# Attention and two mixing FFN layers on one core: token blocks taken layer by layer, weight conversion moved into PSUM and through HBM

## The chip, the cores and the metric

The kernel runs on one core of a Trainium2 chip. The metric is the device time of one execution in microseconds (us), median of the runs; the profile is one execution with the hardware profiler on.

## The reference, cut to what matters

Inputs are float32 for q, k, v, s and the norm's gain, and float64 for the weights (w_ch1, w_ch2 of both layers, U and V). Everything is computed to about float32 precision.

```python
def reference(...):                       # B, H, S, D = 4, 8, 576, 64; d_model 512, FFN 2048
    # causal attention with a bias from a cumulative sum of max(s, 0)
    scores = q @ k.T / 8 + minimum(-(cum_i - cum_j), 0);  attn = softmax(causal(scores)) @ v
    x = concat of the heads               # (4, 576, 512)
    # layer 0
    xn = layer_norm(x) * g_ln
    x = x + maximum(xn @ w_ch1, 0) @ w_ch2
    # layer 1: tokens are mixed with rank 32 first
    u = x + (x.T @ U @ V).T
    return u + maximum(u @ w_ch1b, 0) @ w_ch2b
```

## The kernel before

**Blocks, tiles, steps.** Each of the 4 batches has two token blocks: A (256 tokens) and B (320). A layer's FFN of one block is 16 steps, one for each tile m of 128 hidden units; 2 layers x 8 blocks x 16 = 256 steps. A step is `mlp1` (w1 tile by the normalised tokens, PSUM tile ps) and, LAG = 2 steps later, `mlp2` (w2 tile by the hidden tokens, summed in PSUM over the 16 tiles). To keep float32 precision at the fast matmul format, each operand is split in a high and a low part and three products are made (lines 1026 to 1028 and 1060 to 1062); a step has 24 matmuls of 256 or 320 columns. Between the two, ACT makes hh (L1032) and DVE hl (L1033). The first two steps (FULL_STEPS) run in full precision instead.

**Order of the blocks.** `GROUPS` lists them: A0, A1, A2, B0, A3 in layer 0, then A0 with B0 in layer 1, B1, B2 in layer 0, A1 with B1 in layer 1, and so on. A group takes its first eight tiles for all its blocks, then the other eight; the next group of the layer starts with the eight tiles that are still in SBUF (WSLOTS = 8).

**Attention** of a block (`attn_items`) is spread over the steps given in `AT`, its layer norm (`layer_norm`) comes at the step in `LN`. A0 comes before everything. After layer 0 a block's tokens are mixed with U (`t_items`) and go to HBM (x_dr, t_dr); before its layer 1 they come back (`u_load`, `u_items`). Attention inputs of all blocks but A0 and A1 are first copied within HBM (`bounce`).

**Weights.** A tile has two halves (w1, w2), each 128 x 512 float64 values: 512 KB raw, and 512 KB as high and low part. `w_raw` loads a half into one of three buffers wr. `f64_to_f32` (L460) turns it into float32 in a buffer wt: ACT scales the high word (L466), DVE shifts it left (L469), ACT scales the low word (L471), DVE puts the sign in (L473), POOL adds the low word (L476). `split` then makes the high part w (L352 on ACT or L353 on DVE) and the difference (L357 on DVE or L359 on POOL). `w_split` does this for each half when its turn comes, straight into the w slot that the step uses; a half that is needed again is stored to HBM (w_dr, L519), and later uses load it back from there (L507). 72 halves are converted, 216 loaded back.

**What sets the order.** All work is recorded as operations with an engine (or several to choose from), a priority (the step) and buffers. `Plan.issue` plans them once with prices for each operation, and writes out a fixed order for each engine; every DMA is issued from SP's queue, in that order. Each engine runs its list in order and waits where an operand or a buffer is not ready. PSUM has eight banks: two acc, six ps.

Of the kernel before, what the change touches and what calls it, by code (L numbers as in the profile page):

```python
# [1203 lines left out]
```

## Time and profile before

| | |
|---|---|
| median of 3 runs | 1158.63 us (1158.39 to 1163.0) |
| profiled execution | 1164.62 us, its span 1162.8 us |
| mean granted TensorE clock | 0.973 |
| busy: PE, DVE, ACT, POOL | 1096.6, 618.9, 518.1, 251.3 us |
| matmuls | 7817 |
| DMA | 264.86 MB, 68.8% of 16 engines' span |

Rows of matmuls are longer than the distance between their starts, since they run pipelined; the distance is what a matmul costs. A stretch view gives, for each engine, the time in which it was busy and in brackets how many instructions; "PEclk" is the granted clock as a share of full speed, "DMA" the mean busy share of the 16 DMA engines. Waits are put down to who came last.

### The profile page before, as it was taken

The page shows a single profiled execution, that of the slowest core. Times are in us where ns is not written, and L with a number is a line of the kernel's source. Part 1 is how long each engine was busy: PE and PEld are TensorE (multiplying, and loading weights), DVE is VectorE, ACT ScalarE, POOL GpSimd, SP SyncE. Part 2 cuts the span into 40 slices and gives each one's busy share as a digit, 9 for nine tenths or more (in the row PEclk, how much of TensorE's full clock was granted, in tenths as well). Part 3 has the DMA queues.
Part 4 walks back from the last instruction along what each step waited for, and adds up shares of the span by engine and source line. Part 5 has one row for each costly group of instructions (what it writes and reads, how often), then busy time and mean ns, then how long its engine had stood idle before and what let it go on. Part 6 is the DMA issues. An engine that isn't in the chain of part 4 may idle for free.

```text
span 1162.8 us, 21147 instructions
## 1 busy us (share of the span) xinstructions
PE 1096.6 (94%) x7817; PEld 1035.6 (89%) x7817; DVE 618.9 (53%) x1463; ACT 518.1 (45%) x1212; POOL 251.3 (22%) x391
## 2 busy tenths in 40 slices
PE   8897888999999988798999999999999999999998
PEld 5685788989899987797899989989899999999998
DVE  6877878755554568767845463463441133223122
ACT  7677676645543467556644353342331121112111
POOL 4444344302201144433511030110010000000000
PEclk9998798999999999799899999999999999999999
DMA  7799889596485898869879928955617983611621
GB/s 215 240 358 318 260 271 321 176 274 234 158 302 162 238 336 283 294 221 337 277 245 311 314 63 252 378 188 140 229 47 276 371 284 109 205 46 46 212 79 41
DMA packets 122535, 264.86 MB, mean 228 GB/s; under 512 B 42592, under 2 KB 60544, under 8 KB 122304
## 3 DMA queue, kind: packets, MB, share of 16 engines
q1 hardware_dynamic: 122432, 263.50, 68.8%
q8 instruction: 62, 1.02, 0.3%
q14 instruction: 41, 0.34, 0.1%
HBM read 218.13 MB, written 61.05 MB: 240 GB/s over the span
## 4 chain that ended last, share of the span: by engine, by line
PE 66%; DMA 16%; ACT 5%; DVE 5%; issue 5%; SPq 2%; POOL 2%; POOLq 0%; DVEq 0%; ACTq 0%
PE ps L1026 9%; PE ps L1028 9%; PE ps L1027 9%; PE acc L1060 6%; PE acc L1062 6%; PE acc L1061 6%; DMA t<-cum_dr 4%; PE ps L761 3%; DMA wr<-w1b 3%; PE ps L1062 3%; PE ps L1060 3%; PE ps L1061 3%; PE ps L714 3%; PE ps L665 2%; DMA w<-w_dr 2%
## 5 line engine op out<-in xcount | busy, mean ns | idle before, releaser
L1026 PE MATMUL ps<-xh,w 128*128 128x256 f32 (+1 forms) x1016 | 315.6, 311 | 15.2 <-ACT w L352 5.5
L1027 PE MATMUL ps<-xh,w 128*128 128x256 f32 (+1 forms) x1016 | 306.3, 301 | 7.1 <-DVE w L357 6.9
L1028 PE MATMUL ps<-xl,w 128*128 128x256 f32 (+1 forms) x1016 | 305.4, 301 | 3.4 <-POOL xl L359 3.1
L1033 DVE SCALAR_TENSOR_TENSOR hl<-ps,hh 128x256 fp32r<-128x256 f32 (+1 forms) x254 | 115.6, 455 | 309.9 <-ACT hh L1032 308.7
L1032 ACT ACTIVATE hh<-ps 128x256 fp32r<-128x256 f32 (+1 forms) x254 | 103.3, 407 | 375.2 <-PE ps L1028 373.1
L1060 PE MATMUL acc<-hh,w 128*128 128x256 f32 (+1 forms) x760 | 233.0, 307 | 3.8 <-ACT hh L1032 3.5
L1061 PE MATMUL acc<-hh,w 128*128 128x256 f32 (+1 forms) x760 | 225.7, 297 | 5.1 <-DVE w L357 4.7
L1062 PE MATMUL acc<-hl,w 128*128 128x256 f32 (+1 forms) x760 | 225.9, 297 | 1.1 <-DVE hl L1033 1.1
L1026 PEld LDWEIGHTS ps<-xh,w 128*128 128x128 f32 x1016 | 197.1, 194 | 23.0 <-issue 6.9
L1027 PEld LDWEIGHTS ps<-xh,w 128*128 128x128 f32 x1016 | 197.2, 194 | 9.4 <-DVE w L357 8.8
L1028 PEld LDWEIGHTS ps<-xl,w 128*128 128x128 f32 x1016 | 197.3, 194 | 4.1 <-POOL xl L359 3.5
L1060 PEld LDWEIGHTS acc<-hh,w 128*128 128x128 f32 x760 | 147.8, 195 | 9.5 <-ACT hh L1032 5.0
L1061 PEld LDWEIGHTS acc<-hh,w 128*128 128x128 f32 x760 | 148.2, 195 | 6.8 <-DVE w L357 5.6
L1062 PEld LDWEIGHTS acc<-hl,w 128*128 128x128 f32 x760 | 148.1, 195 | 2.3 <-DVE hl L1033 2.0
L476 POOL TENSOR_TENSOR wt<-wt,wr 128x512 int32<-128x512 int32 (+2 forms) x71 | 98.9, 1393 | 138.1 <-DVE wt L473 78.0
L675 ACT ACTIVATE t<-t,mx 128x256 f32<-128x256 f32 (+4 forms) x144 | 83.2, 579 | 46.1 <-DVE mx L669 28.7
L615 POOL TENSOR_SCALAR_AFFINE_SELECT t<-t 128x128 f32<-128x128 f32 (+2 forms) x128 | 47.7, 378 | 168.6 <-DMA t<-cum_dr 148.3
L1062 PE MATMUL ps<-hl,w 128*128 128x320 f32 x256 | 79.1, 309 | 0.0
L1061 PE MATMUL ps<-hh,w 128*128 128x320 f32 x256 | 79.1, 309 | 0.0
L1060 PE MATMUL ps<-hh,w 128*128 128x320 f32 x256 | 79.1, 309 | 0.0
L714 PE MATMUL ps<-ident,t 128*128 128x128 f32 x400 | 65.4, 280 | 10.3 <-ACT t L688 5.4
L357 DVE TENSOR_TENSOR pB<-ps,pB 128x512 fp32r<-128x512 f32 (+1 forms) x96 | 53.9, 575 | 30.5 <-ACT pB L352 29.6
(137 smaller groups left out, 1585.0 us busy)
## 6 DMA issues: line engine op xcount, KB each, us to landing
w<-w_dr SPq DMA_DIRECT2D x216, 512.0 KB, 6.8
w_dr<-w SPq DMA_DIRECT2D x64, 512.0 KB, 6.1
t<-cum_dr SPq DMA_DIRECT2D x60, 192.0 KB, 6.1
wr<-w1a SPq DMA_DIRECT2D x20, 512.0 KB, 5.6
wr<-w2a SPq DMA_DIRECT2D x20, 512.0 KB, 5.7
t<-cum_dr SPq DMA_DIRECT2D x32, 256.0 KB, 6.2
wr<-w1b SPq DMA_DIRECT2D x16, 512.0 KB, 6.6
wr<-w2b SPq DMA_DIRECT2D x16, 512.0 KB, 5.9
```

The lines of the kernel that those rows point to most:

```text
L357: alts = {"dve": (68 + 1.042 * n, lambda: nc.vector.tensor_tensor(out=out(), in0=a(), in1=b(), op=op))}
L476: P.op(prio, {"pool": (148 + 2.104 * n, lambda: nc.gpsimd.tensor_tensor(out=dst().bitcast(I32), in0=dst().bitcast(I32), in1=pair(0).bitcas ...
L675: act(prio, K, lambda t=t, mx=mx, o=o, K=K, x=x, y=nt * z + x: nc.scalar.activation(t[:, o:o + K], t[:, o:o + K], AF.Exp, bias=mx[:, (1 if ...
L714: nc.tensor.transpose(ps[:, 128 * j:128 * (j + 1)], t[:, c:c + 128], ident.tile)
L1026: nc.tensor.matmul(ps[:, :n], w[:, 0, sl], xh[:, k, :n], start=k == 0, stop=False)
L1027: nc.tensor.matmul(ps[:, :n], w[:, 1, sl], xh[:, k, :n], start=False, stop=False)
L1028: nc.tensor.matmul(ps[:, :n], w[:, 0, sl], xl[:, k, :n], start=False, stop=k == KT - 1)
L1032: act(st - 1000, n, lambda: nc.scalar.activation(hh[:, :n], ps[:, :n], AF.Relu), [ps], [hh], 51)
L1033: dve(st - 1000, n, lambda: nc.vector.scalar_tensor_tensor(out=hl[:, :n], in0=ps[:, :n], scalar=0.0, in1=f(hh[:, :n]), op0=ALU.max, op1=AL ...
L1060: nc.tensor.matmul(a, w[:, 0, sl], hh[:, :n], start=new, stop=False)
L1061: nc.tensor.matmul(a, w[:, 1, sl], hh[:, :n], start=False, stop=False)
L1062: nc.tensor.matmul(a, w[:, 0, sl], hl[:, :n], start=False, stop=last and (z == 1 or blk == "B"))
```

## The change

All blocks go through layer 0 first, A0 and A1 together, then one by one; layer 1 follows in four pairs. Attention of all blocks lies before step 100 now (before: 168), and no step runs in full precision.

The first eight tiles are converted straight into w, as before, and always stored. All other tiles are converted ahead by the new `w_ahead`: raw half into wr (four buffers now), converted, split back into the same wr buffer, stored to HBM; every use in a step is then a load from HBM. The other tiles of layer 0 come at steps 6 to 8, those of layer 1 between steps 37 and 123.

The conversion works in a PSUM bank (one of the six ps) in place of wt: ACT scales the high word into PSUM, ACT scales the low word, one DVE pass shifts and ORs the low word in, one puts the sign in, and the split reads PSUM (so POOL can't take the difference). POOL's add falls away. The v part of the attention inputs is loaded straight into buffers xs and no longer copied in HBM first. The planner's DMA rate is 330 instead of 360 bytes per ns.

```diff
-FULL_STEPS = 2
-
-GROUPS = ((0, "A0"), (0, "A1"), (0, "A2"), (0, "B0"), (0, "A3"), (1, "A0", "B0"), (0, "B1"), (0, "B2"),
-          (1, "A1", "B1"), (0, "B3"), (1, "A2", "B2"), (1, "A3", "B3"))
-
-AT = {"A1": (0, 11), "A2": (11, 24), "B0": (24, 45), "A3": (45, 60), "B1": (64, 100), "B2": (100, 126), "B3": (126, 168)}
-LN = {"A1": 11, "A2": 26, "B0": 45, "A3": 61, "B1": 109, "B2": 127, "B3": 174}
+FULL_STEPS = 0
+
+GROUPS = ((0, "A0", "A1"), (0, "A2"), (0, "A3"), (0, "B0"), (0, "B1"), (0, "B2"), (0, "B3"),
+          (1, "A0", "B0"), (1, "A1", "B1"), (1, "A2", "B2"), (1, "A3", "B3"))
+
+AT = {"A2": (0, 8), "A3": (18, 34), "B0": (26, 48), "B1": (45, 61), "B2": (66, 87), "B3": (76, 100)}
+LN = {"A2": 16, "A3": 36, "B0": 60, "B1": 65, "B2": 90, "B3": 102}
+W0 = (6, 2)
+W1 = (37, 123)
...
-    sb("w", dict(w=2 * WSLOTS, wr=3, wt=2))
+    sb("w", dict(w=2 * WSLOTS, wr=4))
...
-        it["fresh"], it["keep"] = k not in seen, False
-        if k in seen:
-            inst[seen[k]]["keep"] = True
-            if k not in w_dr:
-                w_dr[k] = P.fixed(dr_p.tile([128, 2, 2, 512], F32, name=f"w_dr{k[0]}_{k[1]}"))
-        elif n >= 4:
+        it["fresh"] = k not in seen and n < WSLOTS
+        if k not in seen:
             seen[k] = n
+            w_dr[k] = P.fixed(dr_p.tile([128, 2, 2, 512], F32, name=f"w_dr{k[0]}_{k[1]}"))
...
-        P.op(prio, {
-            "act": (94 + 0.8333 * n, lambda: nc.scalar.activation(dst(), pair(1), AF.Copy, scale=2.0 ** -112)),
-            "dve": (68 + 0.521 * n, lambda: nc.vector.tensor_scalar(out=dst(), in0=pair(1), scalar1=2.0 ** -112, scalar2=None, op0=ALU.mult)),
-        }, [(br, words[1])], [bd], port=True)
-        dve(prio, n, lambda: nc.vector.tensor_scalar(out=dst().bitcast(U32), in0=dst().bitcast(U32), scalar1=3, scalar2=None,
-                                                     op0=ALU.logical_shift_left), [bd], [bd], 0.521)
-        act(prio, n, lambda: nc.scalar.activation(pair(0).bitcast(I32), pair(0).bitcast(U32), AF.Copy, scale=2.0 ** -29),
+        def dv(fn, reads, writes):
+            P.op(prio, {"dve": (68 + 1.042 * n, fn)}, reads, writes, port=not psum)
+
+        alts = {"act": (94 + 0.8333 * n, lambda: nc.scalar.activation(dst(), pair(1), AF.Copy, scale=2.0 ** -112))}
+        if not psum:
+            alts["dve"] = (68 + 0.521 * n, lambda: nc.vector.tensor_scalar(out=dst(), in0=pair(1), scalar1=2.0 ** -112, scalar2=None, op0=ALU.mult))
+        P.op(prio, alts, [(br, words[1])], [bd], port=True)
+        act(prio, n, lambda: nc.scalar.activation(pair(0).bitcast(I32), pair(0).bitcast(U32), AF.Copy, scale=2.0 ** -29 * 0.9374),
             [(br, words[0])], [(br, words[0])])
-        dve(prio, n, lambda: nc.vector.scalar_tensor_tensor(out=dst().bitcast(U32), in0=pair(1).bitcast(U32), scalar=0x80000000,
-                                                            in1=dst().bitcast(U32), op0=ALU.bitwise_and, op1=ALU.bitwise_or),
-            [bd, (br, words[1])], [bd])
-        P.op(prio, {"pool": (148 + 2.104 * n, lambda: nc.gpsimd.tensor_tensor(out=dst().bitcast(I32), in0=dst().bitcast(I32),
-                                                                       in1=pair(0).bitcast(I32), op=ALU.add))},
-             [bd, (br, words[0])], [bd])
+        dv(lambda: nc.vector.scalar_tensor_tensor(out=dst().bitcast(U32), in0=dst().bitcast(U32), scalar=3, in1=pair(0).bitcast(U32),
+                                                  op0=ALU.logical_shift_left, op1=ALU.bitwise_or), [bd, (br, words[0])], [bd])
+        dv(lambda: nc.vector.scalar_tensor_tensor(out=dst().bitcast(U32), in0=pair(1).bitcast(U32), scalar=0x80000000,
+                                                  in1=dst().bitcast(U32), op0=ALU.bitwise_and, op1=ALU.bitwise_or), [bd, (br, words[1])], [bd])
...
         w = it["w", half] = P.buf("w", [128, 2, 512], F32R)
-        t = P.buf("wt", [128, 512])
-        f64_to_f32(prio, 512, lambda: t.tile, lambda: raw.tile, t, raw)
-        split(prio, 512, lambda: w[:, 0], lambda: w[:, 1], lambda: t.tile, [t], [(w, 0)], [(w, 1)])
-        if it["keep"]:
-            load(prio, 128 * 4096, lambda: nc.sync.dma_start(dr[:, half], f(w.tile)), [w], [(dr, half)])
+        t = psum()
+        f64_to_f32(prio, 512, lambda: t.tile, lambda: raw.tile, t, raw, psum=True)
+        split(prio, 512, lambda: w[:, 0], lambda: w[:, 1], lambda: t.tile, [t], [(w, 0)], [(w, 1)], psum=True)
+        load(it["last"], 128 * 4096, lambda: nc.sync.dma_start(dr[:, half], f(w.tile)), [w], [(dr, half)])
+
+    def w_ahead(n, half, gate):
+
+        it = inst[n]
+        prio, dr = it["first"] - 8, w_dr[it["l"], it["m"]]
+        raw, t = w_raw(prio, it["l"], it["m"], half, gate), psum()
+        f64_to_f32(prio, 512, lambda: t.tile, lambda: raw.tile, t, raw, psum=True)
+        split(prio, 512, lambda: raw[:, :512].bitcast(F32R), lambda: raw[:, 512:].bitcast(F32R), lambda: t.tile, [t], [(raw, 0)], [(raw, 1)], psum=True)
+        load(prio, 128 * 4096, lambda: nc.sync.dma_start(dr[:, half], raw.tile.rearrange("p (z c) -> p z c", z=2)), [raw], [(dr, half)])
...
```
```diff
+    ahead = [x for x in sorted({(inst.index(next(it for it in inst if (it["l"], it["m"]) == k)), z) for k in w_dr for z in range(2)}) if x[0] >= WSLOTS]
+    for k, (n, z) in enumerate(ahead):
+        if k >= 2:
+            put(W0[0] + W0[1] * (k - 2) / 16 if k < 16 else W1[0] + (W1[1] - W1[0]) * (k - 16) / 32, lambda p, g, n=n, z=z: w_ahead(n, z, g))
...
+    for _, fn in attn_items(1, "A"):
+        fn(1, None)
+    layer_norm(4, 1, "A")
```

Two places in the engines' lists. The first is SP's queue where the last tiles of the first sixteen come, before (a raw half, then the store of a half that is converted in w):

```order
L488 DMA wr_1656<-w2a 128x1024
L519 DMA w_dr_14_114<-w_1654 128x1024
L486 DMA wr_1685<-w1a 128x1024
L488 DMA wr_1698<-w2a 128x1024
L519 DMA w_dr_14_114<-w_1683 128x1024
L519 DMA w_dr_15_115<-w_1700 128x1024
```

and now, where tiles 8 to 15 go through HBM (`w_dr_12_116` is tile 12 of layer 0):

```order
L484 DMA wr_1670<-w1a 128x1024
L486 DMA wr_1724<-w2a 128x1024
L557 DMA qk_1737<-qkvA_3_139 128x512
L505 DMA w_1750<-w_dr_8_112 128x1024
L577 DMA qkvA_0_140<-qkv_p 128x512
L525 DMA w_dr_12_116<-wr_1562 128x1024
L505 DMA w_1778<-w_dr_8_112 128x1024
L525 DMA w_dr_12_116<-wr_1611 128x1024
L505 DMA w_1795<-w_dr_9_113 128x1024
L505 DMA w_1804<-w_dr_9_113 128x1024
```

The store now starts from wr, and a load of the same half into w follows it in the queue, between raw loads of later tiles.

The second is DVE's list where layer 1's weights are converted. Before, in step 85, in a row with little between:

```order
L469 TENSOR_SCALAR wt_6252<-wt_6252 128x512
L473 SCALAR_TENSOR_TENSOR wt_6252<-wr_6218,wt_6252 128x512
L357 TENSOR_TENSOR w_6270<-wt_6225,w_6270 128x512
L1033 SCALAR_TENSOR_TENSOR hl_6256<-ps_6254,hh_6255 128x256
L469 TENSOR_SCALAR wt_6283<-wt_6283 128x512
L473 SCALAR_TENSOR_TENSOR wt_6283<-wr_6243,wt_6283 128x512
L357 TENSOR_TENSOR w_6292<-wt_6252,w_6292 128x512
```

and now, in step 92, one conversion (`ps_7568`) among the attention of a B block (pB, t, mx):

```order
L359 TENSOR_TENSOR pB_7468<-ps_7506,pB_7467 128x4x128
L695 ISA t_7479,mx_7545<-ps_7530,t_7479 128x512
L695 ISA mx_7545 128x1
L695 ISA t_7500,mx_7580<-ps_7531,t_7500 128x512
L695 ISA mx_7580 128x1
L473 SCALAR_TENSOR_TENSOR ps_7568<-ps_7568,wr_7490 128x512
L475 SCALAR_TENSOR_TENSOR ps_7568<-wr_7490,ps_7568 128x512
L708 RECIPROCAL rc_7598<-sm_7560 128x2
L359 TENSOR_TENSOR pB_7468<-ps_7584,pB_7467 128x4x128
L677 ISA t_7514,mx_7607<-ps_7517,t_7514 128x288
L677 ISA mx_7607 128x1
L359 TENSOR_TENSOR wr_7490<-ps_7568,wr_7490 128x512
```

The conversions of layer 1 moved out of one row of steps and stand singly between the attention's passes, and their result goes to wr and HBM instead of a w that a step waits for.

## Rows read from the trace of the kernel before

**Rows 1.** The page, part 1: busy us (share of the span) xinstructions by engine.

```profile
PE 1096.6 (94%) x7817; PEld 1035.6 (89%) x7817; DVE 618.9 (53%) x1463; ACT 518.1 (45%) x1212; POOL 251.3 (22%) x391
```

**Rows 2.** Timeline of PE, layer 1: start us, row us, line, out<-in, shape.

```profile
1109.99 0.31 PE L1062 MATMUL ps<-hl,w 128*128 128x320 f32 x1
1110.14 0.28 PE L1026 MATMUL ps<-xh,w 128*128 128x256 f32 x1
1110.26 0.28 PE L1027 MATMUL ps<-xh,w 128*128 128x256 f32 x1
```

**Rows 3.** Busy time by stretch: us, engines busy (xcount), PEclk, DMA share, GB/s.

```profile
0.00:137.00 137.00, 114.52 (x729) 91.78 (x730) 104.12 (x266) 97.71 (x243) 60.83 (x68) 0.92 0.86 285
137.00:431.00 294.00, 280.03 (x2143) 266.04 (x2141) 184.91 (x470) 161.28 (x402) 77.92 (x142) 0.99 0.76 243
431.00:567.00 136.00, 115.63 (x747) 106.15 (x747) 106.30 (x215) 89.61 (x183) 61.06 (x73) 0.89 0.85 289
567.00:860.00 293.00, 287.06 (x2020) 273.24 (x2019) 145.71 (x350) 120.79 (x271) 45.76 (x104) 1.00 0.69 222
860.00:1162.80 302.80, 299.34 (x2186) 298.36 (x2184) 77.81 (x165) 48.74 (x115) 5.69 (x6) 1.00 0.48 165
1000.00:1104.50 104.50, 104.50 (x786) 104.50 (x786) 27.61 (x60) 16.93 (x41) 0.88 (x1) 1.00 0.32 108
```

**Rows 4.** The same view, line L1026 alone: PE and PEld busy (xcount), clock, DMA.

```profile
137.00:214.00 77.00, 20.04 (x64) 12.99 (x64) 0.95 0.84 275
137.00:431.00 294.00, 79.09 (x257) 49.64 (x257) 0.99 0.76 243
431.00:567.00 136.00, 31.66 (x96) 20.61 (x96) 0.89 0.85 289
```

**Rows 5.** The same view, all engines, the start cut in two.

```profile
0.00:45.80 45.80, 40.12 (x270) 28.36 (x270) 33.30 (x95) 33.73 (x88) 20.83 (x29) 1.00 0.65 202
45.80:137.00 91.20, 74.39 (x460) 63.42 (x461) 70.82 (x172) 63.98 (x156) 39.99 (x39) 0.88 0.97 327
```

**Rows 6.** PE's waits, 0 to 137 us: who <- for whom: us, times, longest.

```profile
PE ps L1027 <- DVE w L357: 4.9, 4, 2.1
PE ps L1026 <- DVE w L353: 3.6, 2, 2.9
```

**Rows 7.** PE's waits, 431 to 567 us.

```profile
PE ps L1026 <- ACT w L352: 5.5, 3, 3.2
...
PE acc L1061 <- DVE w L357: 3.1, 3, 2.1
...
PE ps L1027 <- DVE w L357: 2.0, 3, 1.0
```

**Rows 8.** Groups by line and shape: xcount | busy us, mean ns | idle before.

```profile
L476 POOL TENSOR_TENSOR wt<-wt,wr 128x512 int32<-128x512 int32 x68 | 96.7, 1423 | 129.4 <-DVE wt L473 72.4 <-ACT wr L471 11.0 <-ACT wt L466 7.3
...
L473 DVE SCALAR_TENSOR_TENSOR wt<-wr,wt 128x512 uint32<-128x512 uint32 x68 | 50.1, 737 | 0.7
...
L357 DVE TENSOR_TENSOR w<-wt,w 128x512 fp32r<-128x512 f32 x60 | 44.5, 742 | 7.3 <-ACT w L352 7.1
...
L466 ACT ACTIVATE wt<-wr 128x512 f32<-128x512 f32 x62 | 41.3, 669 | 20.2 <-DMA wr<-w1b 8.5 <-DVE w L357 4.3 <-DMA wr<-w1a 2.8
...
L469 DVE TENSOR_SCALAR wt<-wt 128x512 uint32<-128x512 uint32 x68 | 38.5, 568 | 20.9 <-ACT wt L466 20.2
...
L357 DVE TENSOR_TENSOR xs<-ps,xs 128x512 fp32r<-128x512 f32 x16 | 11.0, 686 | 7.0 <-ACT xs L352 6.8
```

**Rows 9.** DMA issues: xcount, KB each, median us from issue to landing.

```profile
w<-w_dr SPq DMA_DIRECT2D x216, 512.0 KB, 6.8
...
w_dr<-w SPq DMA_DIRECT2D x64, 512.0 KB, 6.1
...
wr<-w1a SPq DMA_DIRECT2D x20, 512.0 KB, 5.6
```

**Rows 10.** PE's waits, 137 to 431 us: the one for a reload.

```profile
PE ps L1026 <- DMA w<-w_dr: 3.3, 1, 3.3
```

More of the change, by code (lines that the diff above doesn't have):

```diff
@@ L214, in plan @@
             if o.nbytes:
-                o.end = dma_free = max(dma_free, s + 1100) + o.nbytes / 360.0
+                o.end = dma_free = max(dma_free, s + 1100) + o.nbytes / 330.0
             new = []
@@ L540, in load @@
             dt = F32 if self.full else F32R
[L541 to L543 removed]
             if self.full:
[L545 to L547 removed]
+                qk = self.qk = self.v = P.buf("qk", [128, 768], dt)
+                load(prio, 512 * 768, lambda: nc.sync.dma_start(qk.tile, qkv_p[b, p]), [], [qk], gate)
+                return
+            if blk == "A":
+                qk = self.qk = self.v = P.buf("qk", [128, 3, 512], dt)
+            else:
+                qk, v = self.qk, self.v = P.buf("qk", [128, 2, self.k0 + self.kn], dt), P.buf("v", [128, 2 * self.nj, 2, D], dt)
+            src, rd = self.dr.tile, [self.dr]
             if blk == "A":
[L549 removed]
+                load(prio, 512 * 512, lambda: nc.sync.dma_start(f(qk[:, 1]), src[:, :512]), rd, [(qk, "raw")], gate)
             else:
@@ L557, in load, with vt, qkt @@
                 load(prio, 512 * S, lambda: nc.sync.dma_start(f(qk[:, 1, 384:]), src[:, 320:896]), rd, [(qk, "k")], gate)
-            load(prio, 512 * nv, lambda: nc.sync.dma_start(f(v[:, :, 1]), src[:, n1:].rearrange("p (j c) -> p j c", c=D)), rd, [v], gate)
+            self.vr = [P.buf("xs", [128, DM]) for _ in range(2)]
+            for z, a in enumerate(self.vr):
+                v_in = qkv_p[b, p, :, 512 + 128 * z:640 + 128 * z] if blk == "A" else qkv_b[b, 2 * p + z, :, 896:]
+                load(prio, 256 * nv, lambda a=a, v_in=v_in: nc.sync.dma_start(a[:, :nv // 2], v_in), [], [a], gate)
         def bounce(self, prio, gate):
             b, p, blk = self.b, self.p, self.blk
-            w = 768 if blk == "A" else 1536
+            w = 512 if blk == "A" else 896
             dr = self.dr = P.fixed(dr_p.tile([128, w], F32, name=f"qkv{blk}{b}_{p}"))
             if blk == "A":
-                load(prio, 512 * w, lambda: nc.sync.dma_start(dr.tile, qkv_p[b, p]), [], [dr], gate)
+                load(prio, 512 * w, lambda: nc.sync.dma_start(dr.tile, qkv_p[b, p, :, :512]), [], [dr], gate)
                 return
             for z in range(2):
-                load(prio, 256 * 896, lambda z=z: nc.sync.dma_start(dr[64 * z:64 * (z + 1), :896], qkv_b[b, 2 * p + z, 64 * z:64 * (z + 1), :896]),
+                load(prio, 256 * 896, lambda z=z: nc.sync.dma_start(dr[64 * z:64 * (z + 1)], qkv_b[b, 2 * p + z, 64 * z:64 * (z + 1), :896]),
                      [], [(dr, z)], gate)
-                load(prio, 512 * 320, lambda z=z: nc.sync.dma_start(dr[:, 896 + 320 * z:896 + 320 * (z + 1)], qkv_b[b, 2 * p + z, :, 896:]),
-                     [], [(dr, 2 + z)], gate)
+        def vt(self, j, part):
+            if self.full:
+                return self.v[:, 512 + D * j:512 + D * (j + 1)]
+            if self.blk == "A":
+                a = self.v[:, 2].rearrange("p (j t c) -> p j t c", t=2, c=D)[:, j]
+            else:
+                a = self.v[:, j]
+            return a.rearrange("p a c -> p (a c)") if part is None else a[..., part, :]
+        def qkt(self, r, u, c0, c1):
+            return self.qk[r, c0:c1] if self.full else self.qk[r, u, c0:c1]
         def prep(self, prio):
@@ L583, in prep @@
             if self.blk == "A":
-                part(qk, 0, 512, (), "h", None)
+                part(qk, 0, 512, ("raw",), "h", "l")
             else:
@@ L587, in prep @@
                 part(qk, 0, k0, ("z0", "z1", "q0", "q1", "q2"), "qh", "ql")
-            split(prio, 128 * self.nj, lambda: v[:, :, 0], lambda: v[:, :, 1], lambda: f(v[:, :, 1]), [v], [(v, "h")], [v])
+            for z, a in enumerate(self.vr):
+                sl = slice(self.nj * z, self.nj * (z + 1))
+                split(prio, 64 * self.nj, lambda sl=sl: self.vt(sl, 0), lambda sl=sl: self.vt(sl, 1),
+                      lambda a=a: a[:, :64 * self.nj].rearrange("p (j c) -> p j c", c=D), [a], [(v, (z, 0))], [(v, (z, 1))])
         def keys(self, i):
@@ L632, in score @@
             ranges = [(0, 288), (288, S)] if last else [None]
-            rd = [qk] if full or self.blk == "A" else [(qk, x) for x in ("kh", "kl", "k", "qh", "ql", "z0", "z1", "q0", "q1", "q2")]
+            rd = [qk] if full else [(qk, x) for x in ("raw", "h", "l")] if self.blk == "A" else [(qk, x) for x in ("kh", "kl", "k", "qh", "ql", "z0", "z1", "q0", "q1", "q2")]
             nt = len(tick)
@@ L664, in mm @@
                                 r = slice(64 * z, 64 * (z + 1))
-                                nc.tensor.matmul(pss[z][:, p0:p0 + K], qk[r, u, c0:c0 + 128], qk[r, w, k0:k0 + K], start=n == 0, stop=full or n == 2)
+                                nc.tensor.matmul(pss[z][:, p0:p0 + K], self.qkt(r, u, c0, c0 + 128), self.qkt(r, w, k0, k0 + K), start=n == 0, stop=full or n == 2)
                     pe(prio - 500, 1.2 * mm_full(K) if full else 3 * mm_cost(K), mm, rd, [(ps, x) for ps in pss], ts)
@@ L880, in mix_prep_u @@
     def mix_prep_u(prio):
-        raw, u = P.buf("wr", [128, 1024]), P.buf("wt", [128, 512])
+        raw, u = P.buf("wr", [128, 1024]), psum()
         n = 10 * RANK
@@ L895, in mix_prep_u @@
         for z in (0, 2):
[L896 removed]
+            split(prio, n // 2, lambda z=z: u4[:, :, z, :], lambda z=z: u4[:, :, z + 1, :], us, [u], [(u4, z)], [(u4, z + 1)], psum=True)
     v4 = []
@@ L903, in mix_prep_v @@
         for c0 in (0, n):
-            raw, v = P.buf("wr", [128, 1024]), P.buf("wt", [128, 512])
+            raw, v = P.buf("wr", [128, 1024]), psum()
             for z in range(4):
@@ L1134, in mha_ffn_mixer_ffn @@
         w_step(k, None)
+    for n, z in ahead[:2]:
+        w_ahead(n, z, None)
     def side(q):
```

25 lines of the change are left out of this document (9 added, 16 removed).

## The prediction

> **What bounds the kernel now.** I read the busy line of the page first, then stretches cut at step numbers, then what PE waits for. PE is busy 94% of the 1162.8 us [rows 1], but a matmul's row is longer than the time until the next one starts, so a busy PE can still be slow. Its true rate stands in the last part of the run: starts lie 0.12 us apart for 256 columns and 0.1465 us for 320 [rows 2]. A step has 24 MLP matmuls, so a step of an A block costs 2.88 us and one of a B block 3.52 us. There are 128 of each: 819 us. The other matmuls (attention, norms, mixing; counted in the order, fillers left out) are 1458; at 0.12 us, an estimate between the two rates of [rows 2], they are 175 us. PE's own work is therefore about 994 us, and some 170 us of the span is PE waiting or running at a lower clock.
>
> Where that lies is read from stretches cut at steps [rows 3]; L1026 has four matmuls a step, and its counts of 64, 257 (one reaches in from before) and 96 say how many steps a stretch holds [rows 4]:
> - Steps 0 to 15, until 137 us: 14 steps and 2 of full precision, with the attention of A0 and A1, are about 67 us of work. 70 us are lost. In 45.8 to 137 us the DMA engines are 97% busy at 327 GB/s [rows 5], and the largest waits are for converted weights [rows 6]: this start is fed too slowly.
> - Steps 16 to 79 (48 A, 16 B, 597 others): 138 + 56 + 72 = 266 us of work in 294 us, a factor of 1.10. DVE is busy 184.9 us, 0.70 of PE's work.
> - Steps 80 to 103 (16 A, 8 B, 169 others): 94.5 us of work in 136 us, a factor of 1.44. Here layer 1 begins and its 16 weight tiles are converted at once. DVE is busy 106.3 us, 1.12 of PE's work. The granted clock is 0.89. Of the waits, 5.5 + 3.1 + 2.0 us are for weights w that are just being converted [rows 7].
> - Steps 104 to 167: about 270 us of work in 293 us.
> - Steps 168 to 255: 302.8 us. The 32 steps from 1000 to 1104.5 us run without a gap (PE busy 104.5 of 104.5, clock 1.00), DVE at a quarter.
>
> So PE is the limit in the last third, and in the first two thirds a feed that comes late: conversion, attention, DMA.
>
> **The change part by part.** (1) *Cost of a conversion.* Before, a half tile takes two DVE passes (0.568 and 0.737 us) and a difference w (0.742 us, 60 of 72 on DVE), and a POOL add of 1.42 us [rows 8]. DVE: 72 x 1.305 + 60 x 0.742 = 138 us. After: 64 halves, two passes of the L473 kind each and the difference out of PSUM, nearest row 0.686 us: 64 x (1.474 + 0.686) = 138 us. DVE gains nothing here. POOL loses 72 adds of 1.42 us and some 8 differences that are about as long, 114 us, and the order shows it taking other work from DVE instead: by counts of the order times the means of the rows, DVE's summed durations go from 688 (619 busy, since ends overlap [rows 1]) to 650 us, ACT's from 584 to 574, POOL's from 256 to 217. Nothing of this is on the path by itself; it fills the stretches below.
>
> The pass that shifts is now fused with the OR and works in PSUM. The row of the plain shift in SBUF is 0.568 us, that of a two-input pass 0.737 [rows 8]. The Trainium skill, "VectorE: DVE Perf Modes", section "Rules for kernel authors", advises copying a PSUM operand to SBUF first where many operations follow, since a PSUM source runs at 1x: this speaks against the change, which works on a half in PSUM through five passes. No row of before shows a shift from PSUM. By that rule DVE has 64 x 0.17 = 11 us more work than at the shift's speed, 4 us of it in steps 32 to 103, and the sum would end there 4 us later than without it; the 138 us above, from the rows, have the longer pass in them.
>
> (2) *Traffic.* Counted in the order: 288 loads of weight halves (216 reloads, 72 raw) become 256 (192 and 64), 64 stores stay, and v no longer goes through HBM twice: 263 MB become 240 MB. That only matters where DMA is full, at the start.
>
> (3) *Start, steps 0 to 31.* Before, tile 15 is split straight into w. Now tiles 8 to 15 are stored to HBM and read back; the last half of tile 15, needed in step 23, stands behind 56.5 MB on SP's queue. 9.25 MB pass in the first 45.8 us and then 327 GB/s [rows 5]: it lands at about 45.8 + 47.3/0.327 = 190 us, plus a landing of 6.8 us [rows 9] that overlaps the steps before. Steps 24 to 31 (8 x 2.88 + 151 x 0.12 = 41 us) follow: step 32 at about 230 us. Before it came at 214 us [rows 4]. The lower bound is 213 us: the elementwise work up to step 32 is the same (186 against 187 us of summed DVE time), and the store of the fresh tiles 0 to 7 could wait. Upper bound 245 us: the 16 halves share four wr buffers, each held for a landing of 5.6, a conversion of some 4 and a store of 6.1 us [rows 8, 9], 3.9 us a half, 63 us from the time that the first eight tiles are through. I take 230, since in [rows 5] DMA is what is full.
>
> (4) *Dense stretch, steps 32 to 103.* All attention of A3 and B0 to B3 lies here now, and 25 of the 64 conversions: 32 x 2.88 + 40 x 3.52 + 895 x 0.12 = 340 us of PE work. DVE: 310 us of summed durations, about 280 us busy (619 busy for 688 summed, before), 0.82 of PE's work, between the 0.70 and the 1.12 above. What the conversions of layer 1 cost steps 80 to 103 as direct waits goes, since a tile now ends in HBM before its step and is only read back: 10.6 us of waits [rows 7], and the low clock that follows waits (0.89 over 136 us is 30 us at half clock, 1.2 GHz; half of the 15 us lost goes too). So 1.44 becomes (136 - 18)/94.5 = 1.25, and between 1.10 (at 0.70) and 1.25 (at 1.12) a load of 0.82 gives 1.15: 391 us. Bounds: 1.08 (367 us), if the POOL add was what held up the conversions, and 1.27 (432 us). DMA here: from 56.5 MB to at most 170 MB on the queue, 290 GB/s, under the 327 that [rows 5] show; one reload was waited for before, 3.3 us [rows 10].
>
> (5) *Steps 104 to 127:* 24 x 3.52 + 50 x 0.12 = 90.5 us, with little elsewhere: 93 us.
>
> (6) *Layer 1, steps 128 to 255:* four groups of the kind that took 104.5 us [rows 3] = 418 us. The last eight steps took 34.7 us with the drain, 7 us more than in the pattern, and I add 3 us for the entry: 428 us. Bounds 424 and 435.
>
> Sum: 230 + 391 + 93 + 428 = 1142 us of span against 1162.8: 21 us less. The profiled execution took 1164.6 us, the median of the runs is 1158.6; the difference is taken off the median: **1138 us**.
>
> **The rivals.** *Smoother:* conversions off PE's path and POOL nearly free bring the dense stretch to 1.08 (367 us) and the start to 218 us: 1138 - 24 - 12 = 1102 us. For it: the 1.10 of steps 16 to 79 has the last conversions of the start still in it [rows 3]. Against: DVE and ACT are each at 0.8 of PE's work for 390 us.
>
> *Start doubled:* the way through HBM does not run ahead: with the wr buffers at 3.9 us a half and SP's queue in order, step 32 comes at 248 us. Then the change does not do what its words say for tiles 8 to 15, and the rest stays: 1138 + 18 = 1156 us, no change.
>
> *PSUM taken (slower):* each conversion now keeps one of six ps banks through five passes (0.67, two of 0.74, an estimated 0.6, 0.69 [rows 8]: 3.4 us and the waits between), in steps where scores, transposes, p x v and a B block's second pair of sums want banks too. If a bank comes free late, the next PE instruction waits, and SP and DVE behind it. Priced as the weight waits of [rows 7], 1 to 3 us each, 25 conversions at 1.5 us are 37 us: 1175 us. It decides above 20/25 = 0.8 us a conversion. For it: ps holds the matmuls' only way out; against: no row of before shows PE waiting long for a bank.
>
> **How the numbers follow.** Forecast 1138 (1120 to 1150): 0.42. Smoother: 0.22. Start doubled: 0.16. PSUM: 0.20. The range leaves out a tenth at each end: 1104 to 1178, which takes in the bounds of (3) and (4) one at a time. A difference under 0.5% (1152.8 to 1164.4 us) can't be told from none: faster 0.62, same 0.17, slower 0.21.
>
> **What would show it.** Start: step 32 (the first matmul of A2) near 230 us, with PE waiting for w<-w_dr around tile 8 or 15. Dense stretch: steps 32 to 103 in about 390 us, waits for attention (t, pB, qk, v) and hardly any for w; DVE near 280 us. Layer 1: PE without gaps for 428 us at clock 1.00. Wrong, if PE waits for ps banks (matmuls released by a read of ps), if reloads of w are waited for at each group, or if the new PSUM passes take over 0.8 us.

## The result, and the profile after

The changed kernel takes **1129.23 us** (median of 4 runs, 1127.61 to 1131.51) against 1160.55 us of the kernel before beside it: a ratio of 0.973 [0.970, 0.976]. Forecast were 1138 us and a range of 1104 to 1178. The profiled execution took 1127.93 us, its span 1126.1 us.

Busy line of the page (as [rows 1]) and stretches of the changed kernel, cut at its own steps 32, 104 and 128 (as [rows 3]):

```profile
PE 1085.8 (96%) x7862; PEld 1026.9 (91%) x7862; DVE 579.0 (51%) x1378; ACT 502.6 (45%) x1217; POOL 201.4 (18%) x410
```

```profile
0.00:230.10 230.10, 203.12 (x1458) 172.73 (x1459) 166.62 (x446) 159.53 (x433) 70.09 (x149) 0.91 0.81 275
146.10:188.10 42.00, 36.91 (x257) 33.38 (x256) 27.84 (x73) 23.71 (x65) 10.36 (x21) 0.88 1.02 355
230.10:609.80 379.70, 370.38 (x2635) 343.53 (x2634) 265.49 (x631) 245.26 (x558) 115.72 (x243) 1.00 0.82 270
609.80:701.90 92.10, 92.10 (x629) 91.31 (x628) 39.38 (x75) 30.64 (x64) 4.57 (x7) 1.00 0.83 304
701.90:1126.10 424.20, 420.25 (x3147) 419.31 (x3146) 107.52 (x228) 67.19 (x162) 10.99 (x14) 1.00 0.34 113
```

The first column after the times is the length, then PE, PEld, DVE, ACT and POOL busy, the clock, the DMA share and GB/s. The four stages are 230.1, 379.7, 92.1 and 424.2 us; forecast were 230, 391, 93 and 428. From step 32 on the clock is 1.00 and PE has few gaps, though the 379.7 us of steps 32 to 103 still hold only 340 us of work by the prediction's rates. The rest of the old losses lies in the start (clock 0.91), among it steps 16 to 23 (146.1 to 188.1 us), where the DMA engines are full.

PE's largest waits in steps 32 to 103 are for the attention, none for w (compare [rows 7]):

```profile
PE ps L740 <- ACT t L714: 1.8, 1, 1.8
PE ps L672 <- DVE pB L359: 1.4, 1, 1.4
```

The conversion's passes by line and shape (count, busy us, mean ns, idle before), to be read beside [rows 8]:

```profile
L473 DVE SCALAR_TENSOR_TENSOR ps<-ps,wr 128x512 uint32<-128x512 uint32 x64 | 44.6, 697 | 25.4 <-ACT wr L471 24.0 <-DMA w_dr<-wr 0.7
L475 DVE SCALAR_TENSOR_TENSOR ps<-wr,ps 128x512 uint32<-128x512 uint32 x64 | 44.3, 692 | 1.2
...
L359 DVE TENSOR_TENSOR wr<-ps,wr 128x512 fp32r<-128x512 f32 x48 | 33.0, 687 | 8.4 <-ACT wr L354 8.0
```

### The profile page after: what moved, and what is told of

The parts are those of the page before. It is cut to its first block, busy times and chain, and to the rows that moved or that the text cites. A ratio compares the mean times of both kernels' runs of the same rounds, so it can differ in the third digit from the quotient of the medians.

```text
span 1126.1 us, 21112 instructions
## 1 busy us (share of the span) xinstructions
PE 1085.8 (96%) x7862; PEld 1026.9 (91%) x7862; DVE 579.0 (51%) x1378; ACT 502.6 (45%) x1217; POOL 201.4 (18%) x410
## 3 DMA queue, kind: packets, MB, share of 16 engines
q1 hardware_dynamic: 91840, 240.43, 63.3%
q8 instruction: 62, 1.02, 0.4%
## 4 chain that ended last, share of the span: by engine, by line
PE 81%; DMA 5%; DVE 2%; ACT 2%; issue 1%; POOL 0%; SPq 0%; DVEq 0%; POOLq 0%; ACTq 0%
PE ps L1052 11%; PE ps L1054 11%; PE ps L1053 11%; PE acc L1086 8%; PE acc L1088 8%; PE acc L1087 8%; PE ps L787 5%; PE ps L740 3%; PE ps L1088 3%; PE ps L1087 3%; PE ps L1086 3%; PE ps L691 3%; DMA t<-cum_dr 2%; DMA qk<-qkvA 1%; PE ps L672 1%
## 5 line engine op out<-in xcount | busy, mean ns | idle before, releaser
L1052 PE MATMUL ps<-xh,w 128*128 128x256 f32 (+1 forms) x1024 | 311.6, 304 | 4.8 <-ACT xh L354 3.0
L1053 PE MATMUL ps<-xh,w 128*128 128x256 f32 (+1 forms) x1024 | 304.0, 297 | 0.0
L1052 PEld LDWEIGHTS ps<-xh,w 128*128 128x128 f32 x1024 | 195.5, 191 | 10.6 <-ACT xh L354 3.8
L1086 PEld LDWEIGHTS acc<-hh,w 128*128 128x128 f32 x768 | 146.0, 190 | 6.0 <-issue 2.3
L1087 PEld LDWEIGHTS acc<-hh,w 128*128 128x128 f32 x768 | 146.1, 190 | 0.4
L701 ACT ACTIVATE t<-t,mx 128x128 f32<-128x128 f32 (+4 forms) x144 | 83.0, 578 | 40.5 <-DVE mx L695 29.4
L361 POOL TENSOR_TENSOR xl<-x,xh 128x256 fp32r<-128x256 f32 (+1 forms) x17 | 13.2, 801 | 402.0 <-ACT xh L354 402.0
L740 PE MATMUL ps<-ident,t 128*128 128x128 f32 x400 | 64.9, 283 | 11.0 <-ACT t L714 5.2
L695 DVE CUSTOM_DVE_ANT_0 t<-ps,t 128x128 f32<-128x128 f32 (+3 forms) x128 | 58.4, 486 | 30.2 <-POOL t L641 12.8
L641 POOL TENSOR_SCALAR_AFFINE_SELECT t<-t 128x128 f32<-128x128 f32 (+2 forms) x128 | 41.4, 326 | 134.8 <-DMA t<-cum_dr 101.6
```

The costliest lines, as they stand in the source:

```text
L695: dve(prio, K, lambda ps=ps, t=t, mx=mx, o=o, K=K, p0=p0, x=x: nc.vector.tensor_tensor_reduce(out=t[:, o:o + K], in0=ps[:, p0:p0 + K], in1 ...
L701: act(prio, K, lambda t=t, mx=mx, o=o, K=K, x=x, y=nt * z + x: nc.scalar.activation(t[:, o:o + K], t[:, o:o + K], AF.Exp, bias=mx[:, (1 if ...
L740: nc.tensor.transpose(ps[:, 128 * j:128 * (j + 1)], t[:, c:c + 128], ident.tile)
L1052: nc.tensor.matmul(ps[:, :n], w[:, 0, sl], xh[:, k, :n], start=k == 0, stop=False)
L1053: nc.tensor.matmul(ps[:, :n], w[:, 1, sl], xh[:, k, :n], start=False, stop=False)
L1086: nc.tensor.matmul(a, w[:, 0, sl], hh[:, :n], start=new, stop=False)
```

## The experiments

The stages fit the forecast, but that doesn't say which part of the change pays. The prediction's theory: the new order and the conversion ahead pay, the cheaper conversion fills gaps. Its rival: the conversion pays wherever it stands. All runs below are gathered here, first those in the old order of blocks (us; a stage ends where the first matmul of the next stage's first step starts; the last column is the span):

| old order | step 32 at | steps 32-79 | 80-103 | 104-167 | 168-255 | span |
|---|---|---|---|---|---|---|
| before | 214.1 | 216.5 | 136.3 | 293.6 | 302.3 | 1162.8 |
| e10, planned at 330 | 207.7 | 222.4 | 134.4 | 294.1 | 303.4 | 1162.0 |
| e1, new conversion | 196.1 | 214.4 | 121.5 | 294.3 | 302.5 | 1128.8 |
| e5, new, but in SBUF | 200.2 | 213.2 | 123.4 | 292.5 | 302.5 | 1131.8 |

| new order | step 32 at | steps 32-103 | 104-127 | 128-255 | span |
|---|---|---|---|---|---|
| after | 230.1 | 379.7 | 92.1 | 424.2 | 1126.1 |
| e3, planned at 360 | 220.4 | 410.9 | 88.5 | 426.4 | 1146.2 |
| e12, OR in SBUF | 217.6 | 395.8 | 90.3 | 425.1 | 1128.8 |
| e6, old conversion | 236.3 | 391.4 | 91.2 | 424.7 | 1143.6 |
| e2, layer 1 not ahead | 231.7 | 381.2 | 91.3 | 435.2 | 1139.4 |
| e7, five ps banks | 217.3 | 523.5 | 90.5 | 424.3 | 1255.6 |
| e4, tiles 8-15 direct | 201.9 | 393.3 | 91.3 | 425.1 | 1111.6 |
| e9, e4 + OR in SBUF | 212.3 | 400.1 | 92.0 | 423.7 | 1128.1 |
| e11, e4 planned at 345 | 206.9 | 433.2 | 90.3 | 424.6 | 1155.0 |
| e8, e4 with A0 alone first | 200.2 | 423.2 | 90.3 | 425.1 | 1138.8 |

### The conversion by itself

**e1:** the kernel before with nothing but the changed conversion (`f64_to_f32` as in the change):

```diff
-    sb("w", dict(w=2 * WSLOTS, wr=3, wt=2))
+    sb("w", dict(w=2 * WSLOTS, wr=4))
...
-        t = P.buf("wt", [128, 512])
-        f64_to_f32(prio, 512, lambda: t.tile, lambda: raw.tile, t, raw)
+        t = psum()
+        f64_to_f32(prio, 512, lambda: t.tile, lambda: raw.tile, t, raw, psum=True)
```

> The kernel before with the new conversion alone (OR in PSUM, no POOL add, four wr buffers, no wt); order of the blocks, direct conversion of layer 1's tiles and traffic stay as before. Mine: the conversion's DVE time stays near 138 us and PE still waits for tiles that are being converted in steps 80 to 103, so 1150 to 1160 us. Rival (smoother): the conversion is most of the gain, then 1140 us or less and steps 80 to 103 in 125 us or less.

Measured: 1129.36 us, ratio 0.971 [0.968, 0.974]: the rival's case, and 21 us below my range. The conversion alone gives as much as the whole change.

**e5:** of that, only the OR in place of POOL's add; the tile stays in wt, with two wt and three wr buffers as before:

```diff
-        dve(... tensor_scalar(out=dst(), in0=dst(), scalar1=3, op0=logical_shift_left))
+        dv(... scalar_tensor_tensor(out=dst(), in0=dst(), scalar=3, in1=pair(0), op0=logical_shift_left, op1=bitwise_or))
...
-        P.op(prio, {"pool": (... nc.gpsimd.tensor_tensor(out=dst(), in0=dst(), in1=pair(0), op=ALU.add))})
```

> The kernel before with the OR in place of the POOL add, but the half stays in SBUF (two wt, three wr, as before). It splits the 32 us of the run with the whole new conversion. If the POOL pass (1.42 us, and its queue) was what held up the conversions: 1125 to 1137 us, with SP no longer waiting on POOL for a raw buffer. If it was the buffers (ps in place of two wt, four wr) or DVE sharing SBUF with POOL: 1148 to 1160 us.

Measured: 1130.31 us, ratio 0.973 [0.970, 0.976]. So it is neither PSUM nor the fourth wr buffer: leaving out POOL's add is the gain. The run does not tell two ways apart in which the add can cost time: as a link of the conversion's chain, or by slowing DVE's passes beside it. DVE's difference `w<-wt,w` of 128x512 took 742 and 781 ns with the adds (before and e10) and 691 ns in e5, which is 3 to 6 us of DVE's time over its some 60 instances, so for this pass the second is small; no run tests it by itself.

**e10:** the kernel before, planned at 330 in place of 360 bytes per ns, to see what a new plan alone does:

```diff
-                o.end = dma_free = max(dma_free, s + 1100) + o.nbytes / 360.0
+                o.end = dma_free = max(dma_free, s + 1100) + o.nbytes / 330.0
```

> The kernel before, with nothing changed but the rate of DMA by which its planner orders the work: 330 as in the changed kernel. The conversion and the order of layers are the old ones. It shows how far a new plan alone moves the kernel before. Theory (most of the gain of the conversion alone, 31 us, is the conversion and not the luck of its plan): 1160, within 1145 to 1180. Rival (a new plan alone can give that): 1130 or less.

Measured: 1163.61 us, ratio 1.002 [1.000, 1.005]. So the 31 us don't look like the luck of a plan: two plans with the old conversion stand at 1162 us of span, two with the new at 1130. By means of the table, of these 32 us the start gives 210.9 - 198.2 = 12.7, steps 80 to 103 give 135.4 - 122.5 = 12.9, and steps 32 to 79 5.6.

The start up to step 32, of the kernel before and of e5, one row each:

```profile
0.00:214.10 214.10, 184.41 (x1266) 158.14 (x1267) 163.33 (x414) 149.20 (x374) 95.42 (x120) 0.93 0.86 281
```

```profile
0.00:200.20 200.20, 176.46 (x1236) 150.69 (x1237) 166.93 (x417) 135.38 (x350) 56.73 (x101) 0.95 0.89 302
```

Length times GB/s is 60.2 and 60.5 MB (60.4 in e1, 308 GB/s over 196.1 us): the same bytes, moved faster. PE's work is the same in e1 (1271 matmuls for 1266); in e5 it is 30 matmuls less, 3.6 us at 0.12 us each. DMA was not at its limit before, with a share of 0.86; SP's queue stood behind the conversions. The raw loads of the second halves of a tile in that stretch (count: ns, first and last start in us), before and in e5:

```profile
L488 SPq DMA_DIRECT2D wr<-w2a x20: 327/333/522, 2.6 to 177.0; - x20
```

```profile
L487 SPq DMA_DIRECT2D wr<-w2a x20: 327/333/1112, 3.1 to 163.0; - x20
```

The last one is issued 14.0 us earlier, and step 32 comes 13.9 us earlier. With the other two kernels (174.3 us in e10, 159.1 in e1) it holds as well: step 32 follows the last raw load by 37.1, 33.4, 37.0 and 37.2 us in before, e10, e1 and e5. SP's waits in the same stretch (line <- for whom: us, times, longest), before and in e5:

```profile
SPq L486 <- POOL wt L476: 19.8, 11, 4.8
SPq L488 <- POOL wt L476: 15.8, 9, 3.1
```

```profile
SPq L487 <- DVE wt L476: 19.0, 10, 3.7
SPq L485 <- DVE wt L476: 13.0, 9, 3.2
```

A raw load waits until the conversion's last pass has let go of its wr buffer: POOL's add before, DVE's sign pass in e5. These waits alone shrink little, from 35.6 to 32.0 us. All of SP's waits up to step 32, summed over the view, are 127.6 and 122.9 us with the add (before, e10) and 111.6 and 115.6 without (e1, e5): 11.7 us less by the means, 7 of it at raw loads and 6 at stores of converted halves. Each conversion is shorter: 1.42 us of POOL go [rows 8], and the OR adds 0.721 - 0.568 = 0.15 us to the shift. An estimate: 40 halves (20 of each kind, as in the rows above) x 1.27 us / 3 wr buffers = 16.9 us, more than the 12.7 us measured. So the loads do run earlier by what the start gains; that the shorter chain is what lets them is argued from these numbers, not shown by a run of its own.

Steps 80 to 103 in e5, to be read beside the third of [rows 3]:

```profile
413.40:536.80 123.40, 111.38 (x757) 100.95 (x756) 107.28 (x229) 83.55 (x173) 35.53 (x53) 0.96 0.92 321
```

The clock is 0.96 in place of 0.89, and PE's waits for w, summed over the view, are 5.0 us (6.1 in e1) in place of 10.9 (12.2 in e10).

The passes of e5 in SBUF:

```profile
L476 DVE SCALAR_TENSOR_TENSOR wt<-wr,wt 128x512 uint32<-128x512 uint32 x68 | 50.5, 744 | 0.7
L474 DVE SCALAR_TENSOR_TENSOR wt<-wt,wr 128x512 uint32<-128x512 uint32 x68 | 49.0, 721 | 4.6 <-ACT wr L472 3.6 <-issue 0.2 <-ACT wt L468 0.2
```

**e6:** the other way round, the changed kernel with the old conversion (`f64_to_f32` with POOL's add, as in the kernel before):

```diff
-    sb("w", dict(w=2 * WSLOTS, wr=4))
+    sb("w", dict(w=2 * WSLOTS, wr=3, wt=2))
...
-        t = psum()
+        t = P.buf("wt", [128, 512])
```

> The changed kernel with the old conversion (POOL add, wt in SBUF; three wr, since a fourth doesn't fit beside wt). If the conversion is the gain and the rest of the change brings nothing: 1155 to 1170 us. If order and conversion ahead are worth 15 us or more by themselves: 1135 to 1148 us.

Measured: 1149.39 us, ratio 0.989 [0.985, 0.992]. The order and the conversion ahead give 11 us while POOL is in the chain, and nothing on top once it is out (1129.23 against e1's 1129.36). The two parts seem to overlap: each lessens the waits for layer 1's conversions in steps 80 to 103, e1 and e5 to half, the changed kernel to none; no run shows this by itself.

### A plan's own share

**e3:** the changed kernel planned at 360:

```diff
-                o.end = dma_free = max(dma_free, s + 1100) + o.nbytes / 330.0
+                o.end = dma_free = max(dma_free, s + 1100) + o.nbytes / 360.0
```

> The changed kernel, planned with 360 instead of 330 bytes per ns for DMA: nothing else differs, so what it shows is how far a new plan alone moves the time. Mine: within 4 us of 1129. If it is 10 us off, differences of that size in the other runs say nothing.

Measured: 1147.5 us, ratio 0.987 [0.984, 0.990]. My 4 us were a miss: one number of the planner moves the new order by 18 us, with 31 us lost in steps 32 to 103 and 10 won at the start; the old order moved by 3 us. Differences between plans of the new order that are smaller than this say little, which holds for e6 too.

### The way through HBM

**e2:** layer 1's tiles converted straight into w in their own steps:

```diff
-        it["fresh"] = k not in seen and n < WSLOTS
+        it["fresh"] = k not in seen and (n < WSLOTS or it["l"] == 1)
...
-... if x[0] >= WSLOTS]
+... if x[0] >= WSLOTS and inst[x[0]]["l"] == 0]
```

> The changed kernel, but layer 1's 16 tiles are converted straight into w when layer 1 begins (steps 120 to 151) and not ahead through HBM. Mine: PE waits for them there again, 10 to 25 us over the first 32 steps of layer 1, while steps 32 to 103 lose 25 conversions and get at most 10 us shorter: 1135 to 1145 us. Rival (order alone): DVE and ACT are idle by then, so a burst costs nothing and the lighter steps before win: 1119 to 1129 us.

Measured: 1137.57 us, ratio 0.979 [0.974, 0.983]. The place is plain: steps 128 to 159, in e2 and then in the changed kernel:

```profile
704.20:819.70 115.50, 109.32 (x787) 106.25 (x786) 77.66 (x141) 61.44 (x123) 5.33 (x7) 0.99 0.70 261
```

```profile
701.90:806.80 104.90, 104.90 (x786) 104.22 (x786) 28.52 (x60) 18.66 (x44) 2.94 (x4) 1.00 0.42 140
```

The same 786 matmuls run without a gap when the tiles are ready in HBM, and take 10.6 us longer when 77.7 us of DVE work stand among them; of PE's waits there, 3.4 us are for w and 2.3 for hh. Since the other stages agree within 2 us, this part of the change is worth about 10 us in the new order. Steps 32 to 103 hold none of their 25 conversions in e2 (DVE 234.9 us busy for 265.5) and are not shorter for it, 381.2 us for 379.7: conversions that are put there cost PE nothing that shows.

**e4:** tiles 8 to 15 of layer 0 straight into w (and their two early conversions not put ahead):

```diff
-        it["fresh"] = k not in seen and n < WSLOTS
+        it["fresh"] = k not in seen and n < 2 * WSLOTS
...
-        if k >= 2:
-            put(W0[0] + W0[1] * (k - 2) / 16 if k < 16 else W1[0] + (W1[1] - W1[0]) * (k - 16) / 32, ...)
+        if True:
+            put(W1[0] + (W1[1] - W1[0]) * k / 32, ...)
```

> The changed kernel, but tiles 8 to 15 of layer 0 are converted straight into w, as before, and not through HBM and back. Mine (the reload fills DMA at the start): steps 16 to 23 took 42 us for 29 us of work with DMA full at 355 GB/s; without 8.4 MB of reloads they take some 32 us: 1117 to 1123 us. Rival (the start is held up by the attention of A1 and A2, not by DMA): no change, 1126 to 1132 us; or later, 1135 us or more, where conversions into w come too late for a step.

Measured: 1113.86 us, ratio 0.9585 [0.956, 0.961], the fastest of all and 3 us below my range. Step 32 comes at 201.9 us in place of 230.1; the start and its steps 16 to 23:

```profile
0.00:201.90 201.90, 184.99 (x1362) 159.01 (x1363) 159.06 (x433) 144.08 (x389) 50.28 (x115) 0.95 0.80 263
134.70:170.30 35.60, 32.23 (x253) 29.24 (x251) 31.53 (x77) 28.95 (x73) 9.29 (x18) 1.00 1.03 351
```

53.1 MB were moved by then, against 230.1 x 0.275 = 63.3 MB in the changed kernel. The 16 halves read back are 16 x 0.524 = 8.4 MB, 26 us at the 327 GB/s of [rows 5]. But not all of the 28 us is that. The counts of matmuls say that 1458 lie before step 32 in the changed kernel and 1362 here: the plan leaves 96 for later, 11.5 us at 0.12 us each, and steps 32 to 103 are 13.6 us longer for it (2728 matmuls for 2635). In steps 16 to 23, with about the same matmuls, DMA is full in both kernels, moves 12.5 in place of 14.9 MB, and they are 6.4 us shorter; but e9, whose tiles are direct too, takes 45.8 us there, so this is no rule for every plan.

**e11:** the same, planned at 345:

```diff
-                o.end = dma_free = max(dma_free, s + 1100) + o.nbytes / 330.0
+                o.end = dma_free = max(dma_free, s + 1100) + o.nbytes / 345.0
```

> The kernel of the run e4 planned for a rate of 345 in place of 330, nothing else. In the run e3 the rate 360 moved the changed kernel by 18 us. Theory (the first 32 steps are shorter since no ready tile makes the way to HBM and back, whatever the plan): step 32 at 195 to 210, total 1105 to 1130. Rival (the 15 us of e4 were a lucky plan): step 32 over 220 or total over 1130.

Measured: 1156.65 us, ratio 0.996 [0.994, 0.998]. The theory's first half holds (step 32 at 206.9 us), its total doesn't: steps 32 to 103 take 433 us, as the rival would have it. Where they go, steps 88 to 103:

```profile
477.40:640.10 162.70, 136.57 (x800) 119.10 (x798) 106.37 (x258) 87.73 (x197) 42.43 (x89) 0.86 0.54 167
```

```profile
PE ps L740 <- DMA qk<-qkvB: 11.7, 2, 6.2
```

Two late loads of q and k stop PE for 11.7 us, and a mean clock of 0.86 over 162.7 us costs up to 22.8 us at full speed; in e4 the same steps take 112.4 us at a clock of 0.97. DMA is at 0.54 and SP's queue waits 37.2 us there for PE's L740 (18 times, before loads of t): the loads are late by their place in the order, it seems, and not for want of bandwidth. So step 32 does come earlier whatever the plan: at 201.9, 212.3 and 206.9 us in e4, e9 and e11, against 230.1, 217.6 and 220.4 in the changed kernel, e12 and e3, 15.7 us by the means; all four kernels with tiles 8 to 15 direct lie below all six without. But they have 64 matmuls less before step 32, by the means, which is 7.6 of these 15.7 us. And e4's total is a good plan as much as a better design: steps 32 to 103 take 408.9 us in the mean of the first three and 395.5 in that of the others, which gives 13.4 back, so that up to step 104 all but 2 us of the gain is gone.

**e8:** e4 with A0 alone first and A1 spread over steps 0 to 11, as before the change:

```diff
-GROUPS = ((0, "A0", "A1"), (0, "A2"), ...
+GROUPS = ((0, "A0"), (0, "A1"), (0, "A2"), ...
-AT = {"A2": (0, 8), ...
+AT = {"A1": (0, 11), "A2": (11, 24), ...
```

> The changed kernel with tiles 8 to 15 straight into w, and A0 alone first and then A1, as before (attention of A1 and A2 over steps 0 to 24). Mine: in the run with A0 and A1 together PE stands for A1's attention until 107 us (step 8) and its clock falls; taken alone, step 32 comes at 195 us as in the run with the conversion alone instead of 202, but tiles 0 to 7 are read back once more: 1100 to 1113 us. Rival (the same elementwise work stands before step 32 either way): 1110 to 1120 us.

Measured: 1139.06 us, ratio 0.980 [0.977, 0.983], 25 us slower than e4. Step 8 comes 28 us earlier (79.0 against 107.5 us), but step 16 at 139.2 against 134.7 and step 32 at 200.2 against 201.9: A1's attention before step 0 is not what holds the start. Both ranges were missed: 30 us are lost in steps 32 to 103, at 423.2 us for e4's 393.3; why there was not settled.

### PSUM's banks

**e12:** the changed kernel with the OR on tiles in SBUF:

```diff
-    sb("w", dict(w=2 * WSLOTS, wr=4))
+    sb("w", dict(w=2 * WSLOTS, wr=3, wt=2))
...
-        t = psum()
-        f64_to_f32(prio, 512, lambda: t.tile, lambda: raw.tile, t, raw, psum=True)
+        t = P.buf("wt", [128, 512])
+        f64_to_f32(prio, 512, lambda: t.tile, lambda: raw.tile, t, raw)
```

> The changed kernel with the bits' OR on tiles in SBUF in place of PSUM, two wt and three wr buffers, POOL left out of the conversion as in the change. Theory (as in the kernel before, it doesn't matter where the OR is done): 1129, within 1112 to 1146, which is what a new plan alone moves. Rival (PSUM is what gains): about the 1149 of the changed kernel with the old conversion. Second rival (PSUM is what loses, through banks that attention wants): under 1110.

Measured: 1134.53 us, ratio 0.977 [0.974, 0.981]: the theory's case, though its range is as wide as what a plan moves.

**e9:** the same edit on e4.

> The kernel of the run e4 (changed order, tiles 8 to 15 of layer 0 converted straight into SBUF), but with the bits' OR on tiles in SBUF: the six PSUM banks hold nothing of the conversion's, and the planner is told that they are only the matmuls'. Theory (leaving POOL out of the chain is the gain, PSUM as its place costs little at six banks): 1114 us, within 1100 to 1130, step 104 at 585 to 605. Rival (the 25 conversions of steps 32 to 103 cost PSUM banks that the attention wants): steps 32 to 103 shorter by 20 us or more than e4's 393, total under 1095.

Measured: 1131.68 us, ratio 0.976 [0.972, 0.979]: 2 us above the theory's range, with step 104 at 612.4 us for 585 to 605. The rival's freed banks bring nothing that shows (steps 32 to 103 take 400.1 us, not 20 less than 393.3); 18 us more than e4 is within what a new plan alone moved.

**e7:** the changed kernel with five ps banks:

```diff
-    P.pool(ps_p, "ps", 6)
+    P.pool(ps_p, "ps", 5)
```

> The changed kernel with five ps banks instead of six (the sixth stays empty). If conversions that take a bank hold PE up (the slower rival), a bank less costs 20 us or more, 1150 us and up, with waits of PE for readers of ps. Mine: below that, 1129 to 1145 us, seeing that a new plan alone moved the time by 18.

Measured: 1259.78 us, ratio 1.085 [1.078, 1.092]: far over my range, and the slower rival's case. PE's largest waits in steps 32 to 103, which are 144 us longer at a clock of 0.88:

```profile
PE ps L740 <- ACT t L714: 25.4, 7, 6.6
PE ps L1052 <- DVE wr L359: 18.2, 8, 5.3
```

The second row is the rival "PSUM taken" as it was described: mlp1 waits until the split has read a conversion's bank. It exists with five banks; at six the changed kernel shows no such wait among its largest. How much of the 144 us is the conversions' is open: the larger wait is the attention's, and no run has five banks with the conversions in SBUF.

## Why the prediction was right, and where its reasons were not

**Total: right, 9 us too high.** In spans 1142 was forecast and 1126.1 measured; 11.3 of the 15.9 us lie in the dense stretch, 3.8 in layer 1, 0.9 in steps 104 to 127. That the total came so near is in good part luck: the forecast books its gain under the new order and the conversion ahead, and gives the cheaper conversion nothing, while e1 has the whole gain from the conversion alone and e6 has 11 us without it.

**(1) Cost of a conversion: the step that failed.** "Nothing of this is on the path by itself" is wrong: e1 and e5 take 31 us off the kernel before with that part alone, and by e10 this is hardly a plan's luck. The counts of work were good (DVE 579.0 us busy where 650 summed, at the 0.9 of before, make 585; POOL 201.4 where 217 were summed), but busy time was the wrong measure. POOL's add was a link of a serial chain that held a wr buffer and, behind it, SP's queue, and [rows 6, 7] already showed PE waiting for the chain's end. The price was to be looked for on SP's queue, whose waits before step 32 are 127.6 us in all, 35.6 of them for that add, a view that the prediction didn't read.

Of the new passes only the size was open. The two that work in PSUM take 0.697 and 0.692 us in the mean; in SBUF (e5) they take 0.721 and 0.744. The medians of the same lines go the other way, 0.700 and 0.695 against 0.685 and 0.687, so they are about equal. The difference out of PSUM takes 0.687, as taken from the nearest row. The Trainium skill, "VectorE: DVE Perf Modes", section "Rules for kernel authors", advises either to accept 1x for work on a PSUM source or to copy it to SBUF first where many operations follow; for these two-input passes no run here shows a loss in PSUM that a copy would win back.

**(2) Traffic:** 240 MB forecast, 240.43 MB on the queue.

**(3) Start: 230 us, measured 230.1; in part luck.** The reason was a full DMA with the way through HBM in it, and the term's parts fit: step 24 comes at 188.1 us for some 190, and steps 24 to 31 take 42.0 for 41. Steps 16 to 23 run at a DMA share of 1.02, and in e4, with fewer bytes at the same rate, they are 6.4 us shorter, though not in e9. And other plans of the same change reach step 32 at 217.6 (e12) and 220.4 us (e3), so 230 lies at the upper end of what this design gives. The way through HBM costs some 8 us by the means rather than 28, if the matmuls that the plans leave for later are taken off. The forecast wait for w<-w_dr was not seen: among PE's largest waits in the start are t, xh and qk.

**(4) Dense stretch: 391 us, measured 379.7,** a factor of 379.7 / 340 = 1.12 in place of 1.15. No w is waited for and the clock is 1.00, as forecast; DVE is 265 us busy, not 280. The term was reached by a wrong cause in one point: of the 18 us that were credited to converting ahead, about 13 come without it in the old order, from the shorter chain (steps 80 to 103 in e1 and e5). Ahead has its own worth elsewhere, 10 us in steps 128 to 159 (e2). The way from DVE's load to the factor isn't borne out either: e2 has DVE at 0.69 of PE's work in this stretch, the changed kernel at 0.78, and the time is the same. And the stretch moves by 31 us with the planner's rate alone (e3), so that an agreement within 11 us is better than the method can promise.

**(5), (6):** 92.1 us for 93, 424.2 for 428. Layer 1 keeps to 423.7 to 426.4 us in nine of the ten kernels in the new order; only e2 leaves it.

**The rivals.** *Smoother* had half of the true mechanism, that the conversions and POOL were on the path; it was wrong on the place, since the gain was there already without the new order. *Start doubled* didn't come: the bound of 248 us was not reached even in e6 (236.3). *PSUM taken* shows in no wait at six banks and its relief brings nothing (e9, e12, within a plan's spread); at five its wait is real (e7). The prediction had the mechanism and no row for the number of banks at which it sets in.

**Open:** why steps 32 to 103 take from 380 to 433 us in plans at six banks. The matmuls that a plan leaves for after step 32 (2635 to 2774) make up to 17 us of it. Late loads and the clock explain up to 31 of the 50 us by which steps 88 to 103 are longer in e11 than in e4 (11.7 of waits, and 22.8 - 3.4 of clock); for the others no wait stands out. Open is also by which way POOL's add cost the 31 us, as said at e5.
